# One written order for the lead and the first block of a fused attention and two-MoE kernel, with y of two chunks sent through memory

## Chip, core, metric

The program runs on one core of one Trainium2 chip. The metric is the device time of one execution, in microseconds (us). The profiled execution has a time of its own, and a span from its first to its last instruction.

## What is computed

```python
def _attn_ref(q, k, v, a_re, a_im):               # 4 batches, 8 heads, 768 steps, head size 48
    mag = np.sqrt(a_re * a_re + a_im * a_im)
    scale = np.minimum(mag, 0.999) / (mag + 1e-06)
    a_re_n, a_im_n = (a_re * scale, a_im * scale)
    for t in range(S):
        S_re, S_im = (a_re_n*S_re - a_im_n*S_im + kv[t], a_re_n*S_im + a_im_n*S_re)
        y[:, :, t] = einsum('bhd,bhde->bhe', q[:, :, t], S_re)

def _moe_ref(x, w_in, w_out):                     # 3072 tokens, 384 -> 2048 -> 384
    h = x @ w_in
    sp = np.where(h > 20.0, h, np.log1p(np.exp(np.minimum(h, 20.0))))
    return (h * np.tanh(sp)) @ w_out

def _moe2_ref(x, w_a, w_b, w_out):                # 384 -> 1536 -> 384
    return ((x @ w_a) * (x @ w_b)) @ w_out
# attention, its y as 3072 x 384 tokens into the first MoE, and that into the second
```

## The kernel before, in words

**Attention** is cut into 24 chunks of 128 steps: chunk c = 4j + b is the j-th stretch of batch b. A chunk loads `a` (real and imaginary part), `q`, `k`, `v`. From `a` it makes the size and the angle of the decay: squares (`decay_1`), their sum (`decay_sum`), Ln and Exp, `tangent`, `decay_4` (tile `size`), Arctan (`angle`). Two matmuls with a triangle of ones sum both along the steps (`pl` and `pt`, `running_sum`). `decay_exp` and `scale_qk` scale q and k, `reduce_angle` and `trig` give sine and cosine, and `rotate_one` writes the rotated q and k. Then come transposes (`pqT`, `pkT`), scores (`psc`, masked by a predicated copy into `am` or `before_x`), `values` (y) and `outer` (`pu`, the chunk's share of the state `W`). From chunk 4 on a chunk needs its forerunner's last angle and size, which go through memory (`turn_d`, `end_d`), and its y goes through memory too: both halves `yh` and `yl` are written to `yt_d` and read back as `xh` and `xl`. Chunks 0 to 3 make y with the tokens on the partitions (`pyt`), copy it (`yt`), and turn it by three transposes (`px`).

**The first MoE** works in blocks of 512 tokens (block j = chunks 4j to 4j+3), 16 units in each. A unit is `moe1_h` (9 matmuls into an `hps` buffer; the pool `ps_h` has two), `mish_factor` (one VectorE instruction and four on ScalarE), `mish_product` (VectorE, which gives the `hps` buffer back) and, two units later, `moe1_x2`. In block 0 `moe1_x2` is three full float32 matmuls; in the others nine on split halves. The weights come as 8-byte words; each pair of units needs two loads, each decoded by three VectorE instructions (`wf`, `wout`) and split by one copy on ScalarE (`hi`) and one subtraction on GpSimd (`lo`). **The second MoE** follows.

**The order.** The lead, `lead_in`, is the attention of chunks 0 to 3 in a list of steps whose order `in_order` pins on VectorE (DVE), ScalarE (ACT), TensorE (PE) and GpSimd (POOL), not on the load queue (SP). After it the loop over units calls `do_w` for the next weight step and `run_to` for attention slots, and the Tile scheduler may move what it issues.

```python
        for name in """
            sq0 add0 ln0 sq1 add1 ex0 ln1 sq2 tan0 ex1 sq3 ell0 add2 pl0 ln2 ex2 ep0 ell1 tan1 at1 add3 pl1 d1
            ...
            px3 xh2 xh3 xl2 xl3 tan4
        """.split():
            others[name]() if name in others else steps[name[:-1]](int(name[-1]))
        return pipeline(steps1[4:], 2, w_out_1, w_in_1[1:])
```

Of the kernel before, what the change touches and what calls it, by code (L numbers as in the profile page):

```python
# [21 lines left out]
def kernel(  # L22
# [14 lines left out]
    nc = tc.nc  # L37
# [103 lines left out]

    def load_weights(nm, j, src, pool, place, late=False):
# [13 lines left out]
        def decode(first=True, rest=True):  # L156
            if late and first:
                f[0] = wps[0].tile([P, a, b], F32, tag="f", name=f"w{nm}{j}", bufs=NF // 2 + 1)
                whole[nm, j] = f[0], split
                if src.dtype == F32:  # L160
                    nc.vector.tensor_copy(f[0], raw)
                    return
            if src.dtype != F32:
                if not late and first:
                    f[0] = pool.tile([P, a, b], F32, tag="wf32", name="wf32")
                fu, low, high = f[0].bitcast(U32), raw[..., 0], raw[..., 1]
                if first:
                    nc.vector.tensor_scalar(fu, high, 3, 0x3FFFFFFF, ALU.logical_shift_left, ALU.bitwise_and)
                    nc.vector.scalar_tensor_tensor(fu, high, 0xC0000000, fu, ALU.bitwise_and, ALU.bitwise_or)  # L169
                if rest:  # L170
                    nc.vector.scalar_tensor_tensor(fu, low, 29, fu, ALU.logical_shift_right, ALU.bitwise_or)

        def split():
            hi = place(f"w{nm}h{j}", [P, a, b])
            if late:
                lo = wps[0].tile([P, a, b], F32R, tag="f", name=f"w{nm}l{j}", bufs=NF // 2 + 1)
            else:
                lo = place(f"w{nm}l{j}", [P, a, b])
            weights[nm, j] = [hi, lo]
            act(out=hi, in_=f[0], func=AF.Copy)  # L180
            nc.gpsimd.tensor_tensor(lo, f[0], hi.bitcast(F32), ALU.subtract)
# [79 lines left out]
    def in_rows(c, nm):  # L261

        if c < B:
            return pair(c, nm, nm, "h", "a")
        own = QH if nm == "qh" else KH
        if nm == "qh":
            nc.gpsimd.memset(own[:, :, D:], 0.0)
        st[nm, c] = own.rearrange("p (h a) d -> p h a d", a=2)[..., :D]
        return st[nm, c]

    def decay_1(c):
        act(out=pair(c, "s", "qh", "a", "h"), in_=st["a", c], func=AF.Square)
# [173 lines left out]

    def values(c):
# [4 lines left out]
        if not j:  # L452
# [5 lines left out]
        p = st["py", c] = ps_a.tile([P, HH, C], F32, tag="ps", name="py")  # L458
# [11 lines left out]
    def store_y(c):  # L470
        j, b = chunk(c)
        if not j:
# [8 lines left out]
    def store_y2(c):  # L481
        j, b = chunk(c)
        if not j:
            return
        py, yh, yl = st.pop(("y", c))
        nc.vector.tensor_tensor(yl, py, yh.bitcast(F32), ALU.subtract)
        for y, d in zip((yh, yl), yt_d[j]):
            for par in range(2):
# [3 lines left out]
                )  # L492

# [15 lines left out]

    def state(c):  # L510
        j, b = chunk(c)
        if j == NC - 1:
            return
        Wb = W[b][:, :H * D].rearrange("p (h d) -> p h d", d=D)
        us, g = st.pop(("pu", c)), st.pop(("g", c))
        if j:
            nc.vector.tensor_tensor(Wb, Wb, us, ALU.add)
            us = Wb
        (nc.gpsimd if us is Wb else nc.vector).tensor_tensor(Wb, us, g.to_broadcast([P, H, D]), ALU.mult)
# [3 lines left out]
    def read_x(c):  # L523
# [4 lines left out]
        if not j:  # L528
# [70 lines left out]
    def mish_factor(p):  # L599

        m = mp.tile([P, TN], F32, tag="m", name="m")
        nc.vector.tensor_scalar(m, p, 20.0, None, ALU.min)  # L602
        act(out=m, in_=m, func=AF.Exp)
        act(out=m, in_=m, func=AF.Square, bias=bias_one)
        act(out=m, in_=m, func=AF.Ln, scale=0.2, bias=bias_fifth)
# [554 lines left out]
```

## Time and profile before

| | |
|---|---|
| median of 3 runs | 1092.6 us (1092.25 to 1093.58) |
| the profiled execution | 1091.89 us, its span 1090.2 us |
| busy: PE, DVE, ACT, POOL | 1049.1, 655.7, 610.5, 231.4 us |
| granted clock of TensorE, mean | 0.996 |

PE is busy for 96% of the span. "Idle before" is the time in which an engine waited ahead of an instruction, with what ended the wait.

### The profile page before, as it was taken

What the parts mean: (1) busy time and instruction counts of PE and PEld (TensorE: products, weight loads), DVE (VectorE), ACT (ScalarE), POOL (GpSimd) and SP (SyncE); (2) the same over time, 40 slices, a digit from 0 to 9 for tenths busy, and PEclk for the clock granted to TensorE, in tenths of its full rate; (3) what the DMA queues carried; (4) which work ended last, traced back from release to release, by engine and by line L of the source; (5) the groups of instructions that cost most, each with busy time, mean ns of one, the idle gap of its engine ahead of it and who ended that gap; (6) DMA issues with size and microseconds to landing.
All of it is one profiled execution on the core that took longest, in us unless ns stands there. A gap on an engine that the chain in (4) does not pass through costs nothing.

```text
span 1090.2 us, 15919 instructions
## 1 busy us (share of the span) xinstructions
PE 1049.1 (96%) x6060; PEld 874.8 (80%) x6060; DVE 655.7 (60%) x998; ACT 610.5 (56%) x968; POOL 231.4 (21%) x265
## 2 busy tenths in 40 slices
PE   4979999999999999999999999999999999999997
PEld 1956666788888888888877778888888888888886
DVE  6898976787777777777589998532322322422222
ACT  7868887898788887788767842221221222212211
POOL 2122333444334334333331123100000000000000
PEclk9999999999999999999999999999999999999999
DMA  9656652354444343343155366110100100100000
GB/s 199 140 155 170 166 152 66 67 96 86 112 81 81 67 95 79 83 102 79 31 164 182 126 217 211 44 58 1 30 29 1 58 1 1 44 1 1 29 1 32
DMA packets 203549, 90.92 MB, mean 83 GB/s; under 512 B 144781, under 2 KB 187850, under 8 KB 203466
## 3 DMA queue, kind: packets, MB, share of 16 engines
q1 hardware_dynamic: 202410, 89.62, 32.9%
q8 instruction: 50, 0.82, 0.3%
q10 hardware_dynamic: 1056, 0.21, 0.1%
q14 instruction: 33, 0.27, 0.1%
HBM read 72.44 MB, written 17.36 MB: 82 GB/s over the span
## 4 chain that ended last, share of the span: by engine, by line
PE 72%; DVE 12%; ACT 6%; issue 4%; DMA 3%; POOL 2%; SPq 1%; ACTq 0%; DVEq 0%; POOLq 0%
PE x2ps L639 12%; PE ops L719 12%; PE hps L596 12%; PE psa L694 11%; PE psb L694 11%; PE psc L435 3%; PE py L465 3%; ACT m L59 3%; PE pkT L412 2%; PE pqT L412 2%; DVE wf L169 1%; ACT L54 1%; DVE m L602 1%; PE pt L331 1%; PE pu L504 1%
## 5 line engine op out<-in xcount | busy, mean ns | idle before, releaser
L705 DVE TENSOR_TENSOR a_sb<-a_sb,psb 128x512 f32<-128x512 f32 x72 | 49.4, 686 | 224.6 <-PE psb L694 224.6
L59 ACT ACTIVATE m<-m 128x512 f32<-128x512 f32 x192 | 119.4, 632 | 62.5 <-DVE m L602 57.7
L59 ACT ACTIVATE a_sb<-psa 128x512 f32<-128x512 f32 x72 | 42.9, 596 | 162.8 <-PE psa L694 160.7
L59 ACT ACTIVATE ph<-a_sb 128x512 fp32r<-128x512 f32 x72 | 45.4, 631 | 156.7 <-DVE a_sb L705 156.7
L596 PE MATMUL hps<-xh,winh 128*128 128x512 f32 x288 | 118.9, 414 | 7.8 <-DVE gh L613 6.4
L623 POOL TENSOR_TENSOR gl<-m,gh 128x512 fp32r<-128x512 f32 x64 | 83.2, 1300 | 151.7 <-DVE gh L622 128.4
L596 PE MATMUL hps<-xl,winh 128*128 128x512 f32 x288 | 114.0, 396 | 0.0
L596 PE MATMUL hps<-xh,winl 128*128 128x512 f32 x288 | 113.9, 396 | 0.0
L719 PE MATMUL ops<-woh,ph 128*128 128x384 f32 x288 | 97.1, 337 | 0.0
L719 PE MATMUL ops<-woh,pl 128*128 128x384 f32 x288 | 97.1, 337 | 0.0
L719 PE MATMUL ops<-wol,ph 128*128 128x384 f32 x288 | 96.7, 336 | 0.0
L639 PE MATMUL x2ps<-gl,wouth 128*128 128x512 f32 x240 | 94.3, 393 | 2.2 <-DVE gl L623 1.2
L639 PE MATMUL x2ps<-gh,wouth 128*128 128x512 f32 x240 | 94.1, 405 | 1.8 <-ACT gh L59 1.5
L639 PE MATMUL x2ps<-gh,woutl 128*128 128x512 f32 x240 | 94.0, 392 | 0.0
L616 DVE SCALAR_TENSOR_TENSOR m<-m,hps 128x512 f32<-128x512 f32 x80 | 54.7, 684 | 62.3 <-ACT m L59 61.5
L694 PE MATMUL psa<-xh,wal 128*128 128x512 f32 x216 | 85.2, 394 | 0.0
L694 PE MATMUL psa<-xl,wah 128*128 128x512 f32 x216 | 85.1, 394 | 0.0
L694 PE MATMUL psa<-xh,wah 128*128 128x512 f32 x216 | 84.4, 391 | 0.6 <-DVE a_sb L705 0.6
L694 PE MATMUL psb<-xh,wbh 128*128 128x512 f32 x216 | 84.2, 390 | 0.0
L694 PE MATMUL psb<-xh,wbl 128*128 128x512 f32 x216 | 84.2, 390 | 0.0
L694 PE MATMUL psb<-xl,wbh 128*128 128x512 f32 x216 | 84.2, 390 | 0.0
L707 DVE TENSOR_TENSOR pl<-a_sb,ph 128x512 fp32r<-128x512 f32 x72 | 52.0, 722 | 39.0 <-ACT ph L59 39.0
(167 smaller groups left out, 2335.8 us busy)
## 6 DMA issues: line engine op xcount, KB each, us to landing
wraw<-in_moe_w_out_dram SPq DMA_DIRECT2D x14, 768.0 KB
wraw<-in_moe_w_in_dram SPq DMA_DIRECT2D x8, 768.0 KB
a<-in_a_re_dram SPq DMA_DIRECT2D x24, 192.0 KB
q<-in_q_dram SPq DMA_DIRECT2D x24, 192.0 KB
k<-in_k_dram SPq DMA_DIRECT2D x24, 192.0 KB
v<-in_v_dram SPq DMA_DIRECT2D x24, 192.0 KB
wraw<-in_moe_w_a_dram SPq DMA_DIRECT2D x6, 768.0 KB
wraw<-in_moe_w_b_dram SPq DMA_DIRECT2D x6, 768.0 KB
```

What stands on the lines that cost most here:

```text
L59: x = nc.scalar.activation(**kw)
L412: nc.tensor.transpose(p[:, i, :], src[:, h].rearrange("p a d -> p (a d)") if c < B else own[:, h], ident)
L435: nc.tensor.matmul(p[:, i, :], lhsT=st["kT", c, hf][:, i, :], rhs=st["qT", c, hf][:, i, :], start=True, stop=True)
L465: nc.tensor.matmul(p[par * 64:(par + 1) * 64, i, :], lhsT=w[:, col:col + 64], rhs=x[:, first + par, :], start=(n == 0), stop=(n == len(ter ...
L596: nc.tensor.matmul(p, lhsT=w[:, kk, :], rhs=x[:, kk, :], start=(i == 0), stop=(i == len(ops) - 1))
L616: nc.vector.scalar_tensor_tensor(m, m, 2.5, p, ALU.subtract, ALU.mult)
L623: (nc.vector if on_act else nc.gpsimd).tensor_tensor(gl, m, gh.bitcast(F32), ALU.subtract)
L639: nc.tensor.matmul(x2ps[m], lhsT=w[:, ms], rhs=x, start=(f == 0 and i == 0), stop=(f == NF - 1 and i == len(terms) - 1),)
L694: nc.tensor.matmul(p, lhsT=w[:, kk, :], rhs=x[:, kk, :], start=(i == 0), stop=(i == len(ops) - 1))
L705: nc.vector.tensor_tensor(a_sb, a_sb, pb, ALU.mult)
L707: nc.vector.tensor_tensor(lo, a_sb, hi.bitcast(F32), ALU.subtract)
L719: nc.tensor.matmul(ops_t[t], lhsT=x[:, tsl], rhs=w, start=(f == 0 and i == 0), stop=(f == NF2 - 1 and i == 2),)
```

## The change

Lead, block 0 and the first two units of block 1 are one list of names, which `run` turns into steps. Each engine keeps the list's order, the load queue SP now too. A name like `rq2` is a step of chunk 2; a name with a dot is one of a weight load (`w.3` issues load 3; `da`, `dc`, `db` are its three decodes, `hi` and `lo` its split; `so`, `sl` split a kept w_out) or of a unit (`h.0`, `mn`, `ma`, `mb`, `pr`, `x.0`). So weight decodes, unit 0 and the attention of chunks 4 to 9 stand where the list has them. Three other things are new: y of chunks 0 and 1 is made as column tiles and sent through memory, as it is for later chunks; the squares of chunks 1 to 3 run on DVE instead of ACT; and the kept w_out tiles have a buffer by name (`kept`) instead of nine that go round.

```diff
     def decay_1(c):
+        if c in (1, 2, 3):
+            nc.vector.tensor_tensor(pair(c, "s", "qh", "a", "h"), st["a", c], st["a", c], ALU.mult)
+            return
         act(out=pair(c, "s", "qh", "a", "h"), in_=st["a", c], func=AF.Square)
...
+    BY_MEMORY = (0, 1)
     def values(c):
-        if not j:
+        if not j and c not in BY_MEMORY:
             p = st["py", c] = ps_l.tile([P, H, D], F32, tag="pl", name="pyt")
...
-            terms = [(W[b], qT[hf]), (vt, am[hf])]
+            terms = [(W[b], qT[hf]), (vt, am[hf])] if j else [(vt, scored(c)[hf])]
...
-    weights1 = lead_in()
-    last, after_lead = in_order(first, (E.DVE, E.Activation, E.PE, E.Pool)), traced()
+    run("""
+            a0 sq0 add0 a1 sq1 add1 ln0 ex0 tan0 at0 a2 sq2 add2 ln2 ex2 ln1 ex1 ell0 pl0 ep0 w.1 da.1 dc.1
+            ...
+            xh3 ht3 xl3 close da.4 at5 cy5 ca5 ep5 dc.4 db.4 ou2 tk14 ck14 tq14 cq14 io1 h.0 mn.0 ma.0 w.5
+            da.5 re2 dc.5 db.5 pt5 h.1 mn.1 tk04 ou3 mb.0 pr.0 he5 w.6 a6 re5 st2 st3 open so.0 sl.0 ma.1 mb.1
+            ...
+    """)
+    last, after_lead = in_order(first, (E.DVE, E.Activation, E.PE, E.Pool, E.SP)), traced()
+    slot[0] = 50
...
-    for ui in range(len(units) + lag):
-        if ui == 3:
-            behind(after_lead, last)
+    for ui in range(18, len(units) + lag):
```

**TensorE, end of the lead and the first units.** Before (`pu` is `outer`; `hps` with `winh_476` is units 0 and 1, with `winh_585` units 2 and 3; `x2ps` is `moe1_x2`; the last `pl` and `pt` are chunk 4's):

```order
L532 MATMUL px<-ident,yt 128x128 x6
L504 MATMUL pu<-v,kh 64x48 x11
L596 MATMUL hps<-xh,winh_476 128x512 x2
L504 MATMUL pu<-v,kh 64x48 x6
...
L331 MATMUL pl<-size,csum 128x384
L504 MATMUL pu<-v,kh 64x48 x47
L331 MATMUL pt<-a,tsum 128x384
L596 MATMUL hps<-xh,winh_585 128x512
...
L639 MATMUL x2ps_801<-gh,wout_485 128x512
```

and after the change, from chunk 5's `pl` on (`winh_208` is units 0 and 1, `winh_325` units 2 and 3):

```order
L349 MATMUL pl<-size,csum 128x384
L568 MATMUL px<-ident,yt 128x128 x6
L534 MATMUL pu<-v,kh 64x48 x16
L434 MATMUL pkT<-ident,khp 128x128 x4
L434 MATMUL pqT<-ident,qhp 128x128 x4
L632 MATMUL hps<-xh,winh_208 128x512
...
L349 MATMUL pt<-a,tsum 128x384
...
L434 MATMUL pkT<-ident,khp 128x128 x4
L534 MATMUL pu<-v,kh 64x48 x16
L434 MATMUL pqT<-ident,qhp 128x128 x4
L632 MATMUL hps<-xh,winh_325 128x512
...
L688 MATMUL x2ps_859<-gh,wout_264 128x512
```

Three chunks' `pu`, chunk 4's sums and half its transposes, and chunk 5's `pl` now stand ahead of unit 0; behind unit 1 stand 4 + 16 + 4 small matmuls ahead of unit 2.

**VectorE, between the last `xl` of block 0 and the first instructions of the units** (`L602`, later `L638`, reads `hps`). Before:

```order
L544 TENSOR_TENSOR xl<-px,xh 128x3x128 x2
L291 TENSOR_TENSOR a<-a,khp 128x384
L297 TENSOR_SCALAR qhp<-qhp 128x384
L298 SCALAR_TENSOR_TENSOR size<-khp,qhp 128x384
L168 TENSOR_SCALAR wout_611<-wraw 128x768
L519 TENSOR_TENSOR W_129<-pu,g 128x384
L169 SCALAR_TENSOR_TENSOR wout_611<-wraw,wout_611 128x768
L168 TENSOR_SCALAR wf_627<-wraw 128x768
L171 SCALAR_TENSOR_TENSOR wout_611<-wraw,wout_611 128x768
L169 SCALAR_TENSOR_TENSOR wf_627<-wraw,wf_627 128x768
L602 TENSOR_SCALAR m<-hps 128x512
```

and after the change:

```order
L300 TENSOR_TENSOR a<-a,khp 128x384
L415 TENSOR_TENSOR qhp<-q,a 128x16x48
L415 TENSOR_TENSOR khp<-k,a 128x16x48
L580 TENSOR_TENSOR xl<-px,xh 128x3x128 x2
L172 TENSOR_SCALAR wout_690<-wraw 128x768
L321 SCALAR_TENSOR_TENSOR a<-size,a 1x384
L174 SCALAR_TENSOR_TENSOR wout_690<-wraw,wout_690 128x768
L176 SCALAR_TENSOR_TENSOR wout_690<-wraw,wout_690 128x768
L638 TENSOR_SCALAR m<-hps 128x512
L172 TENSOR_SCALAR wf_749<-wraw 128x768
L174 SCALAR_TENSOR_TENSOR wf_749<-wraw,wf_749 128x768
```

Nine instructions stood between them before, four now; chunk 4's rotation (`L415`) and chunk 5's `tangent` (`L300`) have gone ahead of the last `xl`.

**The load queue, between the last loads of the lead and unit 0.** Before (`g` is the read of `end_d`, `size<-turn_d` the read of the carried angle):

```order
L153 DMA wraw<-in_moe_w_in_dram 128x3x512
L308 DMA size<-turn_d_90 1x384
L220 DMA q<-in_q_dram 128x8x48
L220 DMA k<-in_k_dram 128x8x48
L220 DMA a<-in_a_re_dram 128x8x48
L220 DMA a<-in_a_im_dram 128x8x48
```

and after the change, from the second read of chunk 4's `g` on:

```order
L396 DMA g<-end_d_86 48x8x1 x2
L316 DMA size<-turn_d_91 1x384
L572 DMA xh<-yt_dh_68 128x3x128
L572 DMA xl<-yt_dl_69 128x3x128
L157 DMA wraw<-in_moe_w_in_dram 128x3x512
L396 DMA g<-end_d_88 48x8x1 x2
```

The read of chunk 1's `xh` and `xl`, which did not exist before, stands behind the read of chunk 5's carried angle; chunk 0's stands three rows ahead of these.

## Rows read from the trace of the kernel before

**Rows 1.** The page: busy time by engine.
```profile
PE 1049.1 (96%) x6060; PEld 874.8 (80%) x6060; DVE 655.7 (60%) x998; ACT 610.5 (56%) x968; POOL 231.4 (21%) x265
```

**Rows 2.** Windows up to 180 us: PE, PEld, DVE, ACT, POOL busy; clock; DMA.
```profile
0.00:5.90 5.90, 0.00 (x0) 0.00 (x0) 0.12 (x3) 2.12 (x2) 5.26 (x18) 1.00 0.86 134
5.90:13.60 7.70, 3.06 (x4) 1.00 (x4) 5.01 (x12) 6.87 (x10) 1.25 (x7) 1.00 1.27 236
13.60:52.78 39.18, 33.26 (x239) 28.01 (x238) 33.98 (x56) 33.44 (x58) 2.21 (x10) 1.00 0.84 154
66.40:83.89 17.49, 15.55 (x42) 9.92 (x43) 17.01 (x27) 10.19 (x15) 3.13 (x2) 0.80 0.44 141
```

**Rows 3.** Windows from unit 0's first matmul on, to 180 us and beyond.
```profile
52.78:180.00 127.22, 118.65 (x769) 81.49 (x767) 107.05 (x152) 96.98 (x147) 37.74 (x34) 0.97 0.58 150
180.00:330.00 150.00, 145.70 (x1045) 121.73 (x1044) 112.95 (x183) 129.41 (x207) 63.93 (x80) 1.00 0.42 88
330.00:1090.20 760.20, 748.47 (x4011) 642.60 (x4009) 396.61 (x595) 341.62 (x550) 120.98 (x118) 1.00 0.24 66
```

**Rows 4.** What PE waited for: us in total, times, longest.
```profile
PE hps L596 <- DVE gh L613: 6.4, 3, 3.3
```

**Rows 5.** Timeline of PE: start, us, instruction, idle before.
```profile
25.81 1.06 PE L412 MATMUL pqT<-ident,qhp 128*96 128x128 f32 x4
30.35 0.60 PE L412 MATMUL pqT<-ident,qhp 128*96 128x128 f32 x4
...
66.40 0.50 PE L596 MATMUL hps<-xh,winh 128*128 128x512 f32 x1 [3.33 <-DVE gh L613]
67.07 0.63 PE L596 MATMUL hps<-xh,winl 128*128 128x512 f32 x1
...
72.96 0.39 PE L596 MATMUL hps<-xl,winh 128*128 128x512 f32 x1
...
79.44 0.50 PE L596 MATMUL hps<-xh,winh 128*128 128x512 f32 x1 [1.94 <-DVE gh L613]
```

**Rows 6.** Timeline of DVE around the first units.
```profile
53.52 2.05 DVE L297 TENSOR_SCALAR qhp<-qhp 128x384 f32<-128x384 f32 x1
...
60.09 0.69 DVE L602 TENSOR_SCALAR m<-hps 128x512 f32<-128x512 f32 x1
...
67.13 0.55 DVE L385 TENSOR_TENSOR q<-q,size 128x384 f32<-128x384 f32 x1
67.60 0.95 DVE L171 SCALAR_TENSOR_TENSOR wout<-wraw,wout 128x768 uint32<-128x768 uint32 x1
68.47 0.55 DVE L386 TENSOR_TENSOR k<-k,size 128x384 f32<-128x384 f32 x1
...
78.44 0.35 DVE L297 TENSOR_SCALAR qhp<-qhp 128x384 f32<-128x384 f32 x1
```

**Rows 7.** Timeline of POOL, the split of the second w_in load.
```profile
53.36 1.95 POOL L181 TENSOR_TENSOR winl<-wf,winh 128x768 fp32r<-128x768 f32 x1 [8.80 <-ACT winh L59]
```

**Rows 8.** The chain of waits at full clock: start, us, what.
```profile
87.94 0.44 PE pkT L412 x4
88.38 0.65 PE pt L331 x2
89.02 2.07 PE hps L596 x9
...
92.88 2.58 PE x2ps L639 x6
95.45 1.90 PE py L465 x32
97.35 0.71 PE pu L504 x24
```

**Rows 9.** Load queue: chunk 4's y written and read back.
```profile
98.02 0.30 SPq L489 DMA_DIRECT2D yt_dh<-yh  x1
...
103.89 0.52 SPq L536 DMA_DIRECT2D xh<-yt_dh  x1
```

More of the change, by code (lines that the diff above doesn't have):

```diff
@@ L154, in load_weights, with decode @@
         f = [raw]
-        def decode(first=True, rest=True):
-            if late and first:
-                f[0] = wps[0].tile([P, a, b], F32, tag="f", name=f"w{nm}{j}", bufs=NF // 2 + 1)
+        def decode(part=None):
+            if late and part in (None, 0):
+                f[0] = kept(j, F32, f"w{nm}{j}")
                 whole[nm, j] = f[0], split
-                if src.dtype == F32:
+            if src.dtype == F32:
+                if late and part in (None, 0):
                     nc.vector.tensor_copy(f[0], raw)
[L162 to L181, printed above, removed]
+                return
+            if not late and part in (None, 0):
+                f[0] = pool.tile([P, a, b], F32, tag="wf32", name="wf32")
@@ L830, in behind, with run @@
                 tc.add_manual_dep(x, last[x.engine], no_sync, reason="after the lead")
-    def lead_in():
-        for c in range(B):
-            load_a(c)
-        decode, split = steps1[0]()
-        for c in range(B):
-            load_qk(c)
-        for c in range(B):
-            load_v(c)
-        decode_2, split_2 = steps1[1]()
-        run_to(slot[0] + 1)
-        w_in_1 = steps1[2]()
-        def size(c):
-            decay_4(c)
-            split_ell(c)
+    units = [(b, f) for b in range(NB) for f in range(NF)]
+    ready, lag = {}, 2
+    hs, ms, loads = {}, {}, {}
+    late_pools = {}
+    def run(names):
         def turned(c):
@@ L887, in lead_in @@
-        """.split():
-            others[name]() if name in others else steps[name[:-1]](int(name[-1]))
-        return pipeline(steps1[4:], 2, w_out_1, w_in_1[1:])
+        parts = {
+            "w": lambda n: loads.update({n: steps1[n - 1]()}),
+            "da": lambda n: loads[n][0](0), "dc": lambda n: loads[n][0](1), "db": lambda n: loads[n][0](2),
+            "hi": lambda n: loads[n][1](0), "lo": lambda n: loads[n][1](1),
+            "so": lambda n: whole["out", n][1](0), "sl": lambda n: whole["out", n][1](1),
+            "h": lambda n: hs.update({n: moe1_h(*units[n], ps_h)}),
+            "mn": lambda n: ms.update({n: mish_bound(hs[n])}),
+            "ma": lambda n: mish_grow(ms[n]), "mb": lambda n: mish_shrink(ms[n]),
+            "pr": lambda n: ready.update({n: mish_product(hs.pop(n), ms.pop(n), units[n][0])}),
+            "x": lambda n: moe1_x2(*units[n], *ready.pop(n)),
+        }
@@ new lines, in run, with end_lead, end_first @@
+        for name in names.split():
+            kind, dot, n = name.partition(".")
+            if name in late_pools:
+                late_pools[name]()
+            elif dot:
+                parts[kind](int(n))
+            else:
+                steps[name[:-1]](int(name[-1]))
+    def end_lead():
+        nonlocal mp
+        lead.close()
+        mp = allp.enter_context(tc.tile_pool(name="mp", bufs=3))
+    def end_first():
+        nonlocal ps_x
+        tail.close()
+        ps_x = w1.enter_context(tc.tile_pool(name="ps_x", bufs=1, space=PSUM))
+        wps.append(allp.enter_context(tc.tile_pool(name="wp1", bufs=NF)))
@@ L976 @@
             moe2_out(*units[ui - lag], *pend.pop(ui - lag), ps_o, p2)
+    behind(after_lead, last)
     allp.close()
```

214 lines of the change are left out of this document (131 added, 83 removed).

## The prediction

> **What bounds the kernel now.** First the page: PE is busy 96% of the span, DVE 60%, ACT 56% [rows 1]. PE is the bound, so a change can only win where PE stands idle or runs at its lower clock. The windows say where that is. From 180 us to the end PE is busy 145.7 of 150.0 and 748.5 of 760.2 us [rows 3]. Behind unit 17 both programs have the same number of matmuls (only neighbours change places), so I leave those 910.2 us as they are, with 1.5 us either way for units that start in another state. All else lies in the first 180 us, of which the trace of before makes three parts:
>
> - Up to 52.78 us, where unit 0 starts, PE is idle for 16.5 us and DVE is busy 0.1 + 5.0 + 34.0 = 39.1 us. DVE's idle time there is 5.8 us until the first data, 2.7 us to 13.6 and 5.2 us after that [rows 2].
> - From 52.78 to 180 PE is busy 118.65 of 127.22 us [rows 3], so 8.6 us idle.
> - Inside that, from 66.40 to 83.89, the granted clock is 0.80 on average [rows 2]: after a wait of 3.33 us and again after one of 1.94 us, matmuls that take 0.39 us elsewhere take 0.63 [rows 5]. That is the 1.2 GHz level instead of 2.4, and costs 0.20 x 17.5 = 3.5 us.
>
> The waits of the last two points are mostly one: an `hps` matmul behind `gh`, 6.4 us in 3 times [rows 4]. `ps_h` has two buffers, and a third unit must wait until the first unit's product is made. That product was late since DVE came to unit 0's first instruction only at 60.09 [rows 6], some 5 us after unit 0's matmuls (2.07 us of work from 52.78 on [rows 8], with some of `pu` between them): the decodes of the next two loads and a stalled `L297` stood ahead of it.
>
> So T, the time at which unit 18 starts, is now 52.8 + 115.1 of PE work at full clock (118.65 - 3.5) + 12.1 lost (8.6 + 3.5) = 180.0. A new T is made of the same three terms.
>
> **Term 1: when unit 0 starts.** In the new list it stands behind more work. On DVE the following is new ahead of the last `xl`: the squares of chunks 1 to 3 and chunk 4's rotation, 5 instructions of 128x768; `tangent` of chunks 4 and 5, chunk 4's carried angle, two scalings, chunk 5's sum, two states `W` and two sizes, 10 of 128x384; two `tensor_scalar`, and three of chunk 4's `reduce_angle`; and two `yl` in place of two `xl`. From start to start a 128x384 costs 0.47 us and a 128x768 0.87, a `tensor_scalar` 0.35 when nothing stalls it [rows 6]; for the other three I take 0.5 each, and `yl` against `xl` is worth 0.3. Sum: 4.35 + 4.7 + 0.7 + 1.5 + 0.3 = 11.5 us. So DVE has 39.1 + 11.5 = 50.6 us to do before unit 0. The three squares leave ACT (at 33.4 of 39.2 us nearly as full as DVE in that window [rows 2]).
>
> What idle time comes on top? The 5.8 + 2.7 us at the start stay, since they wait for the first loads: 59.1. The 5.2 us after that are waits of a chunk's next step on PE or ACT; the list puts chunk 4's and 5's steps between those of chunks 2 and 3. If all are filled, unit 0 starts at 59.1, if none at 64.3. I take half: 61.7.
>
> A stall adds to the upper end. `L297` took 2.05 us at 53.52 and 0.35 at 78.44 [rows 6]; the long one ended with the split that POOL ran from 53.36 to 55.31 [rows 7]. Two splits stand in the lead after the change too, so up to 1.7 us more: 66.0. The Trainium skill (GPSIMD Engine Reference, Specifications) says that GpSimd's SBUF interfaces are shared with VectorE, with contention for instructions with two SBUF inputs or in a two-port mode. The trace agrees: 1.7 us lost here. By that rule the new squares, which have two SBUF inputs each and have left ACT, can stall as well, at most for both splits' whole time, 3.9 us, and unit 0 would start at 68.2; by the row it is 66.0.
>
> PE in the lead is no limit at full clock: it was busy 36.3 us before unit 0 [rows 2] and gets 5.1 us more (below), 41.4 of 61.7. y of chunks 0 and 1 by column tiles shortens it (`py` with its two terms takes 1.90 us [rows 8], one term about half, and the transposes fall away), which I count at nothing. What that costs instead is a way through memory: for chunk 4 the first write was issued at 98.02 and the read at 103.89 [rows 9], 5.9 us later. Chunks 0 and 1 are written first in the list and have ten microseconds and more for it, so also nothing, if the queue lets them (rival 3).
>
> **Term 2: PE's work from unit 0 to unit 18.** Moved ahead of unit 0 are 8 transposes (0.44 for 4), two `pl` and one `pt` (0.65 each), and 37 of the 64 `pu` matmuls that stood behind its start (0.71 for 24 records, two records a matmul: 2.2) [rows 8]. That is 0.9 + 1.95 + 2.2 = 5.05. Units cost the same as before: 2.07 for `hps`, 2.58 for `x2ps` [rows 8]. So 115.1 - 5.0 = 110.1.
>
> **Term 3: what PE loses in between.** It lost 12.1 us. The list takes away what made unit 0's product late: only the decode of one load (three instructions, under 2.5 us) stands on DVE between the last `xl` and unit 0's bound, while PE computes unit 0 for 2.07 us; and three small steps (0.44 + 0.95 + 0.44) stand on PE between units 1 and 2, where it stood idle for 3.33. DVE and ACT have room: 107.05 and 96.98 us of work in 127 [rows 3], less what has moved ahead. I take 1.7 us for one stretch at the lower clock, as each of the two before cost, and 1.3 us for waits: 3.0. Bounds: 0 and 12.1.
>
> **Sum.** T = 61.7 + 110.1 + 3.0 = 174.8 instead of 180.0: 5.2 us less. The profiled execution took 1091.89 us, so 1086.7; it lies 0.7 us under the median of the runs shown, which I leave inside the range.
>
> **Rivals.**
>
> 1. *More is filled.* Unit 0 at 59.1 and PE loses nothing: T = 169.2, 1081.1 us. For it: a list that holds loads, decodes and attention together can place each step for all engines. Against it: DVE would have to work without a wait for 46 us, and it was idle 5.2 of 39 so far. Chance 0.20 for a gain of over 8 us.
> 2. *No change.* The 5.2 us of DVE's waits and a POOL stall stay, unit 0 at 66.0, loss 3: T = 179.1, 1091.0 us. An engine that must keep a written order waits for a late step with all behind it. Chance 0.14 for within 0.2% of 1092.6 (2.2 us, about what a measurement of this kernel can tell from no change).
> 3. *Slower: the two `hps` buffers go on holding PE.* All of block 0 is in written order now, on SP too. A weight load waits there for its buffer, and the read of chunk 1's `xh` stands behind the read of chunk 5's angle, which waits for a matmul of the lead. If a late load or decode delays products as before, PE loses 12.1 us again while its start is 9 us later: T = 61.7 + 110.1 + 12.1 = 183.9, 1095.8 us. It decides from a loss of 8.2 us on. For it: three waits of this kind now. Against it: what stood ahead of them has been moved. Chance 0.07.
> 4. *Slower: the clock.* In the lead of before, transposes went from 1.06 us for four at 25.81 to 0.60 at 30.35 [rows 5], the step from 1.2 to 2.4 GHz; before that PE had run with few gaps. The new lead spreads nearly the same PE work over 9 us more. If the clock stayed down until unit 0, the 23 us from 30 to 52.78 would take 46: unit 0 at 13.6 + 33.3 + 5.1 + 23 = 75.0 at worst, T = 188, 1100 us. The Trainium skill (TensorE: Matmul & The Clock Gate, on HAM oscillation) says that an array which pauses between bursts falls back to half rate; rows 5 show that behind both waits. But at half rate PE would have few gaps left in the lead and rise again. Chance 0.04.
>
> **Chances and range.** My forecast, a gain of 2.2 to 8 us (1084 to 1089.7), has 0.55. With rival 1 that is faster 0.75; same 0.14; slower 0.11. The range that leaves out 2 in 10 reaches from rival 1's time, less the 1.5 us for the units behind 18 and a little more, to rival 3's: 1079 to 1095.5.
>
> **What would show it.** In the new profile: unit 0's first `hps` at 59 to 66 us; DVE's busy time ahead of it near 51 us; unit 18's first at 169 to 180; waits of `hps` for `gh` well under 6.4 us and at most one stretch at the lower clock after 60 us; the windows behind unit 18 as before. I am wrong if unit 0 starts past 70, which would be the load queue or the clock; if PE waits for `gh` as often as now; or if units behind 18 wait for attention that the list has left late.

## The result, and the profile after

The changed kernel takes 1108.16 us (median of 4 runs, 1106.77 to 1108.59), the kernel before beside it 1092.42 us: a ratio of 1.0141, 95% interval 1.0123 to 1.0158. It is slower by 15.7 us, where the sum had a gain of 5.2.

First the page, busy time by engine, to be held against [rows 1]:

```profile
PE 1049.0 (95%) x6054; PEld 871.6 (79%) x6054; DVE 662.6 (60%) x1001; ACT 612.2 (55%) x965; POOL 236.5 (21%) x265
```

TensorE's work is the same, VectorE's has grown by 6.9 us, and the span is 16 us longer. The windows of the changed kernel (length; PE, PEld, DVE, ACT, POOL busy; granted clock; DMA share; GB/s) say where. Unit 0's first `hps` starts at 60.2, unit 18's at 196.9:

```profile
0.00:60.20 60.20, 38.87 (x323) 29.10 (x324) 52.55 (x92) 49.91 (x76) 12.80 (x36) 1.00 0.86 167
60.20:120.00 59.80, 50.45 (x257) 32.41 (x256) 57.25 (x71) 42.36 (x62) 22.84 (x15) 0.97 0.51 147
120.00:142.41 22.41, 12.60 (x74) 8.45 (x73) 8.25 (x14) 11.59 (x18) 1.84 (x1) 0.70 0.58 142
142.41:196.90 54.49, 52.98 (x352) 37.20 (x352) 32.77 (x50) 41.03 (x62) 11.50 (x13) 1.00 0.38 84
196.90:1106.30 909.40, 894.12 (x5054) 764.46 (x5052) 511.81 (x778) 467.28 (x750) 187.49 (x201) 1.00 0.28 72
```

Behind unit 18 nothing has changed (909.4 us, 910.2 before). Unit 0 starts 1.5 us ahead of its forecast (61.7). Between them, in 136.7 us instead of 127.2 [rows 3], PE is idle for 136.7 - 116.0 = 20.7 us, in two places of different kinds: from 60 to 120, where DVE is busy for 57.25 of 59.80 us, and from 120 to 142, where nobody is busy and the clock is at 0.70.

What PE, DVE and the load queue (SPq) waited for, from 60 to 200 us (us in total, times, longest):

```profile
PE pu L534 <- DMA v<-in_v_dram: 9.4, 2, 8.0
PE x2ps L688 <- DVE gh L662: 7.1, 4, 3.2
PE hps L632 <- DVE gh L662: 3.4, 3, 2.2
...
DVE wf L172 <- DMA wraw<-in_moe_w_in_dram: 10.8, 1, 10.8
...
SPq L228 <- DVE qhp L415: 27.6, 2, 14.1
```

The wait of [rows 4] has halved (6.4 to 3.4). Two others have come: for `v`, and for `gh` ahead of `x2ps`. The load queue's last row is the key to the first of them; its timeline (start, us, instruction) shows it in place:

```profile
107.15 0.37 SPq L157 DMA_DIRECT2D wraw<-in_moe_w_out_dram  x1
121.12 0.37 SPq L228 DMA_DIRECT2D a<-in_a_re_dram  x1
121.54 0.58 SPq L228 DMA_DIRECT2D a<-in_a_im_dram  x1
122.17 0.51 SPq L387 DMA_DIRECT2D end_d<-size  x1
...
125.74 0.47 SPq L157 DMA_DIRECT2D wraw<-in_moe_w_in_dram  x1
126.31 0.43 SPq L157 DMA_DIRECT2D wraw<-in_moe_w_out_dram  x1
...
127.15 2.02 SPq L247 DMA_DIRECT2D v<-in_v_dram  x1
```

For 13.6 us the queue issues nothing. It stands at the load of chunk 7's `a` (`a7`), whose buffer is free only when DVE has rotated chunk 5's q (`rq5`); loads 15 and 16 and a `v` stand behind it in the list. (The other of the two waits, 14.1 us for chunk 8's `a`, costs next to nothing: it falls behind 142, where PE is idle for 1.5 of 54.5 us.) DVE's timeline has that rotation at 120.09, and then a hole:

```profile
63.19 0.69 DVE L638 TENSOR_SCALAR m<-hps 128x512 f32<-128x512 f32 x1 [0.43 <-DMA g<-end_d]
...
71.76 0.68 DVE L638 TENSOR_SCALAR m<-hps 128x512 f32<-128x512 f32 x1
...
76.87 0.68 DVE L662 SCALAR_TENSOR_TENSOR gh<-m,hps 128x512 f32<-128x512 f32 x1
77.47 1.62 DVE L172 TENSOR_SCALAR wout<-wraw 128x768 uint32<-128x768 uint32 x1
79.13 2.47 DVE L174 SCALAR_TENSOR_TENSOR wout<-wraw,wout 128x768 uint32<-128x768 uint32 x1
81.52 0.68 DVE L638 TENSOR_SCALAR m<-hps 128x512 f32<-128x512 f32 x1
...
120.09 0.95 DVE L415 TENSOR_TENSOR qhp<-q,a 128x768 f32<-128x768 f32 x1
131.80 0.56 DVE L172 TENSOR_SCALAR wf<-wraw 128x768 uint32<-128x768 uint32 x1 [10.76 <-DMA wraw<-in_moe_w_in_dram]
```

The first row is unit 0's bound, its first instruction on DVE. The rows from 71.76 to 81.52 show the other place. A decode at 77.47 takes 1.62 us and one at 79.13 takes 2.47, where their like take 0.56 (at 131.80) and, as in [rows 6], 0.95. POOL at that time:

```profile
71.02 2.50 POOL L188 TENSOR_TENSOR winl<-wf,winh 128x768 fp32r<-128x768 f32 x1 [1.58 <-ACT winh L59]
...
76.11 2.57 POOL L188 TENSOR_TENSOR woutl<-wout,wouth 128x768 fp32r<-128x768 f32 x1 [2.59 <-ACT kT L59]
78.63 2.15 POOL L188 TENSOR_TENSOR winl<-wf,winh 128x768 fp32r<-128x768 f32 x1
```

Each stretched decode ends about its own length after POOL's subtraction has ended (78.68, 80.78), while `m<-hps` at 71.76, also under a subtraction, keeps its 0.68 us. Unit 3's bound, at 81.52, stood behind both; its matmuls were done at 78.0. PE's timeline has the consequence:

```profile
85.81 2.84 PE L688 MATMUL x2ps<-gh,wout 128*128 128x512 f32 x6 [3.19 <-DVE gh L662]
...
89.19 0.39 PE L632 MATMUL hps<-xh,winh 128*128 128x512 f32 x1
...
97.25 0.50 PE L632 MATMUL hps<-xh,winh 128*128 128x512 f32 x1 [2.23 <-DVE gh L662]
...
98.05 0.62 PE L632 MATMUL hps<-xh,winh 128*128 128x512 f32 x1
...
134.13 1.95 PE L534 MATMUL pu<-v,khp 128*64 128x48 f32 x32 [8.04 <-DMA v<-in_v_dram]
```

Behind the wait of 2.23 us the matmuls of 0.39 us take 0.62 for a while (1.2 instead of 2.4 GHz), as in [rows 5]; behind that of 3.19 us they keep 0.39. The long stretch at the lower level falls into the hole from 120 to 142 (0.70 in the windows).

So two theories. **A**: the load queue in written order makes the hole from 120 to 142 us. **B**: DVE is full from 60 to 120 us, so bounds and products come late. A rival within B asks what fills it: decodes that the list has too early, or the stretches under POOL.

### The profile page after: what moved, and what is told of

It is laid out like the page before. It is cut to its first block, busy times and chain, and to the rows that moved or that the text cites. A ratio compares the mean times of both kernels' runs of the same rounds, so it can differ in the third digit from the quotient of the medians.

```text
span 1106.3 us, 15891 instructions
## 1 busy us (share of the span) xinstructions
PE 1049.0 (95%) x6054; PEld 871.6 (79%) x6054; DVE 662.6 (60%) x1001; ACT 612.2 (55%) x965; POOL 236.5 (21%) x265
## 4 chain that ended last, share of the span: by engine, by line
PE 64%; DVE 13%; ACT 7%; DMA 6%; issue 6%; POOL 2%; SPq 1%; DVEq 0%; ACTq 0%; POOLq 0%
PE ops L772 12%; PE psa L747 12%; PE psb L747 12%; PE x2ps L688 11%; PE hps L632 9%; ACT m L59 3%; PE py L490 3%; PE psc L457 2%; PE pkT L434 1%; DVE wf L176 1%; DVE m L638 1%; PE pqT L434 1%; ACT L54 1%; DVE wf L174 1%; PE pu L534 1%
## 5 line engine op out<-in xcount | busy, mean ns | idle before, releaser
L758 DVE TENSOR_TENSOR a_sb<-a_sb,psb 128x512 f32<-128x512 f32 x72 | 49.4, 686 | 224.8 <-PE psb L747 224.8
```

Of the source, the lines that this page charges most:

```text
L758: nc.vector.tensor_tensor(a_sb, a_sb, pb, ALU.mult)
```

## The experiments

All medians in one table, with the ratio to the kernel before run beside them. That one's median was 1092.42 us beside the changed kernel, 1090.94 beside 1 to 4, 1091.26 beside 5 to 8, and 1090.57 to 1090.86 beside the others, so between these groups a difference is good to a microsecond or so only. "Unit 0" and "unit 18" are the starts of their first `hps` in the profiled execution, and PE busy is what the window between them says. A profiled execution is one of several: that of 9 took 1.9 us more than the median, that of 10 took 3.4 us less.

| kernel | median us | ratio (95%) | unit 0 | unit 18 | between | PE busy |
|---|---|---|---|---|---|---|
| changed | 1108.16 | 1.0141 (1.0123 to 1.0158) | 60.2 | 196.9 | 136.7 | 116.0 |
| 1 `a7` later | 1097.62 | 1.006 (1.0043 to 1.0077) | 60.4 | 187.2 | 126.8 | 114.0 |
| 2 queue free | 1096.94 | 1.006 (1.0043 to 1.0077) | 60.2 | 185.5 | 125.3 | 113.6 |
| 3 decodes later | 1116.83 | 1.0243 (1.0225 to 1.0261) | 60.2 | 204.8 | 144.6 | 115.5 |
| 4 ten decode steps out | 1087.79 | 0.9972 (0.996 to 0.9983) | 60.2 | 176.0 | 115.8 | 110.7 |
| 5 = 2 + 3 | 1110.13 | 1.0169 (1.015 to 1.0188) | 60.1 | 201.1 | 141.0 | 120.0 |
| 6 eleven subtractions out | 1086.69 | 0.996 (0.9946 to 0.9974) | 60.1 | 176.8 | 116.7 | 110.9 |
| 7 squares on ACT | 1100.85 | 1.009 (1.0073 to 1.0107) | 64.1 | 190.5 | 126.4 | 115.5 |
| 8 y without memory | 1102.97 | 1.0124 (1.0101 to 1.0147) | 64.7 | 191.0 | 126.3 | 115.3 |
| 9 quarters | 1091.86 | 1.0008 (0.9999 to 1.0017) | 60.0 | 182.5 | 122.5 | 112.8 |
| 10 six swaps | 1097.38 | 1.0056 (1.0042 to 1.007) | 60.1 | 184.5 | 124.4 | 112.8 |
| 11 subtractions on DVE | 1109.60 | 1.0176 (1.0162 to 1.0191) | 60.4 | 198.4 | 138.0 | 118.8 |
| 12 before, eleven out | 1086.06 | 0.9955 (0.9941 to 0.997) | 52.4 | 173.0 | 120.6 | 116.1 |
| 13 = 10 + all quarters | 1090.77 | 0.9997 (0.9988 to 1.0007) | 61.2 | 181.1 | 119.9 | 112.5 |
| 14 before, quarters | 1088.78 | 0.998 (0.997 to 0.9989) | 52.4 | 177.9 | 125.5 | 118.0 |
| 15 eighths | 1092.78 | 1.0017 (1.0008 to 1.0027) | 60.1 | 181.5 | 121.4 | 112.6 |
| 16 all quarters | 1091.61 | 1.0005 (0.9995 to 1.0014) | 61.7 | 181.7 | 120.0 | 112.4 |
| 17 three steps ahead | 1093.30 | 1.0024 (1.0014 to 1.0034) | 60.3 | 183.1 | 122.8 | 114.1 |

### 1 and 2. The load queue

```diff
-dc.13 pr.6 db.13 w.14 a7 yt4 pl6 ep6 he6 re6 h.7 mn.7
+dc.13 pr.6 db.13 w.14 yt4 pl6 ep6 he6 re6 h.7 mn.7
...
-so.5 so.6 cq05 cq15 w.15 w.16 da.15
+so.5 so.6 cq05 cq15 w.15 w.16 a7 da.15
```

> The changed kernel with one entry of the list moved: the load of chunk 7's `a` stands behind chunk 5's `rotate` (just behind the load w.16) instead of before it, so that the load queue no longer waits for that buffer with w.15, w.16, `v` and the `g` reads behind it. Theory A (the written order of the load queue makes the hole from 120 to 142 us): unit 18 starts some 13 us earlier than 196.9 (9.8 us of PE's idle time and 3.3 of its lower clock go), so 1093 to 1097 us, DVE's wait of 10.8 us for the load in L172 and PE's wait of 8.0 us for `v` are gone, and PE's loss before 120 us, about 11, stays. Theory B (DVE is full in block 0 since decodes stand units ahead of their use, and that sets the pace throughout): the DVE work comes later by what the hole was, gain under 3 us, 1105 us or more.

```diff
-    last, after_lead = in_order(first, (E.DVE, E.Activation, E.PE, E.Pool, E.SP)), traced()
+    last, after_lead = in_order(first, (E.DVE, E.Activation, E.PE, E.Pool)), traced()
```

> The changed kernel with the load queue (SP) taken out of the engines that keep the list's order; the four other engines keep it. Theory A: the load of chunk 7's `a` no longer holds up the loads behind it, the hole from 120 to 142 us goes, so 1093 to 1097 us as with the load moved. If the written order of the queue served for something else (loads that now go ahead take a transfer's place), it is less. Theory B: under 3 us of gain, 1105 us or more.

One name moved in the list takes 10.5 us off (9.1 if each is counted from the kernel before beside it; unit 18 starts 9.7 earlier), and the free queue 11.2. Theory A holds. The hole is gone from the queue of the first (timeline; load 15 now goes at 111.56 instead of 125.74):

```profile
111.56 0.41 SPq L157 DMA_DIRECT2D wraw<-in_moe_w_in_dram  x1
115.86 0.39 SPq L157 DMA_DIRECT2D wraw<-in_moe_w_out_dram  x1
120.02 0.37 SPq L228 DMA_DIRECT2D a<-in_a_re_dram  x1
```

What is left is the loss before 120 us. PE's waits in the first kernel, from 60 to 200 us:

```profile
PE x2ps L688 <- DVE gh L662: 8.0, 6, 3.2
PE hps L632 <- DVE gh L662: 1.4, 2, 1.2
```

### 3 and 5. Loads and decodes later

```diff
-w.8 da.8 dc.8 h.3 mn.3 db.8 h.4 mn.4 x.2
+w.8 h.3 mn.3 h.4 mn.4 da.8 dc.8 db.8 w.10 x.2
...
-w.12 da.12 dc.12 mb.5 pr.5 hi.11 lo.11 so.3 h.6 mn.6
+mb.5 pr.5 so.3 h.6 mn.6 da.10 dc.10 db.10 w.12
```

(Shown are two of nine places. The decodes of the weights 8 to 16 go one to five units later in the list, most of them two or three; their loads move less, and those of weights 10 and 11 stand a little earlier than they did.)

> The load of `a` of chunk 7 behind chunk 5's `rotate`, that of chunk 8 behind chunk 6's, and the loads and decodes of the weights 8 to 16 written two to three units later, just ahead of the unit that first needs them; all else as in the changed kernel. Theories A and B together: the hole from 120 to 142 us goes (13 us), and with DVE's decodes out of the way the waits of `hps` and `x2ps` between 80 and 120 us shrink from about 11 to 5 us or less: 1085 to 1091 us. A alone: as with the load of chunk 7 moved alone, 1093 to 1097. If the late decodes come too late, `hps` waits for its weight and the time is over 1097.

Far off: 19 us slower than with chunk 7's load moved alone, where 6 to 12 less was expected. With the queue in written order, `v` now stands behind weight loads that wait for their decodes; of PE's waits (from 60 to 200 us) the longest kind is

```profile
PE pu L534 <- DMA v<-in_v_dram: 18.5, 2, 11.5
```

So the same edit with a free queue:

> The kernel with the later loads and decodes of weights 8 to 16, now with the load queue (SP) free of the list's order (the two edits of the two earlier runs together). If the later decodes themselves were right and only the queue, in written order, held `v` back behind weight loads (PE waited 7.0 and 11.5 us for `v` in that run): PE's waits for `v` are gone and the gaps of `hps` and `x2ps` between 80 and 120 us are down to half, 1087 to 1092 us, against 1096.9 for the free queue alone. If not the place of the decodes but DVE's total of work in block 0 sets the pace: 1095 to 1098 us. If late decodes make units wait for their weights: over 1098 us.

PE no longer waits for `v`, but the time is still 13 us over that of the free queue alone. DVE is less busy (40.4 us from 60 to 120) and PE loses more. So the decodes of the changed kernel are not simply too early. A weight must go from DVE through ACT's copy and POOL's subtraction before PE can use it, and POOL now waits for the copies; but no wait of PE names a weight, its longest are for `gh` (POOL, then PE, from 60 to 200 us). What delays `gh` there is not shown:

```profile
POOL winl L188 <- ACT winh L59: 37.7, 5, 18.6
...
PE x2ps L688 <- DVE gh L662: 10.2, 4, 3.9
```

### 4 and 6. What fills DVE

```diff
-... db.6 ... da.6 dc.6 so.1 db.6 so.2 ...
+... db.6 ... da.6 so.1 db.6 so.2 ...
```

(The same for `dc.5` to `dc.14`; `a8` also stands behind `rq6`.)

> The load of `a` of chunks 7 and 8 behind the `rotate` that frees its buffer, and the second of the three decode steps (the sign bit of the weight) left out for weights 5 to 14: 10 DVE instructions, about 9 us of DVE's work between 60 and 120 us; these weights lose their sign. Theory B (DVE sets the pace there): 5 to 9 us less than with chunk 7's load moved alone, 1085 to 1090 us, and PE's idle time between 60 and 120 us at 5 us or less. Theory A alone (the rest of the loss comes from the order, not from DVE's load): within 2 us of the kernel with chunk 7's load moved, 1093 to 1097 us.

The time falls by 9.8 us, and unit 18 starts 11.2 us earlier than in the first run. B holds. But the ten steps are only some 9.5 us of it: DVE is busy for 15.1 us less between unit 0 and unit 18 (99.86 against 84.79, below), so about 5.6 us of stretches went with them, and this run alone does not tell work from stretches. Then the stretches alone, with all decodes in place:

```diff
+            if part == 1 and nm + str(j) in ("in2", ..., "in6", "out0", ..., "out5"):
+                weights[nm, j].append(weights[nm, j][0])
-            if part in (None, 1):
+            elif part in (None, 1):
```

> The kernel with chunk 7's load moved, and POOL's subtraction that makes a weight's low part left out for the weights of eleven loads that units 4 to 13 use (their high part is used twice; 11 POOL instructions of about 2 us). Seven DVE instructions between 60 and 120 us were 9.8 us longer in all than their like, each while such a subtraction ran. If those stalls are a large part of what fills DVE: they vanish, DVE does the same work about 9 us sooner, unit 18 starts 8 to 11 us earlier than 187.2, 1086 to 1090 us. If DVE's own work sets the pace and the stalls only take its spare time: under 3 us of gain, 1095 us or more.

10.9 us, as much as the whole of B. No DVE instruction has been taken out here, only POOL's subtractions beside them. Windows from unit 0 to unit 18, of the first run, then of 4, then of 6:

```profile
60.40:187.20 126.80, 114.02 (x681) 75.51 (x679) 99.86 (x133) 95.02 (x141) 35.67 (x29) 0.99 0.51 130
```
```profile
60.20:176.00 115.80, 110.67 (x681) 75.41 (x679) 84.79 (x123) 94.57 (x141) 34.19 (x29) 1.00 0.55 142
```
```profile
60.10:176.80 116.70, 110.91 (x682) 75.51 (x680) 87.72 (x133) 94.95 (x141) 12.00 (x17) 1.00 0.56 142
```

DVE's 133 instructions take 99.86 us with the subtractions beside them and 87.72 without, and the way from unit 0 to unit 18 is 10.1 us shorter. A rival would be that PE had waited for the low parts themselves, which 6 does not make; but in the first run no wait of PE between unit 0 and unit 18 names a weight's low part. PE runs at full clock in both of the lower rows, which also gives its true work: 110.7 to 110.9 us.

### 7 and 8. The two other parts of the change undone

```diff
     def decay_1(c):
-        if c in (1, 2, 3):
+        if False:
```

> The kernel with chunk 7's load moved, and the squares of chunks 1 to 3 back on ACT: one part of the change undone. By the first term of the prediction they cost DVE 3 x 0.87 = 2.6 us ahead of unit 0: unit 0 at 57.8 instead of 60.4 if DVE sets the start of unit 0, and 1095 us; if ACT, busy 50 of 60 us there, takes them as late as DVE did, unit 0 stays at 60.4 or goes up to 63 and the time is 1097.5 to 1100 us.

```diff
-    BY_MEMORY = (0, 1)
+    BY_MEMORY = ()
...
-cq12 xl0 ell4 re0 a5 sq5 sy0 cy4 ou0
+cq12 px0 xh0 xl0 ell4 re0 a5 sq5 cy4 ou0
```

(The same for chunk 1; the writes and reads of both, `sy` and `io`, are out.)

> The kernel with chunk 7's load moved, and y of chunks 0 and 1 made as for chunks 2 and 3, by transposes on PE and copies on ACT, without the way through memory: the other part of the change undone, the list otherwise as it was. If the way through memory is hidden and spares PE and ACT work in the lead: unit 0 starts 1 to 3 us later than 60.4, 1098.5 to 1100.5 us. If the writes and reads of y hold loads up in the queue: unit 0 at 58 to 60, 1094 to 1097 us.

Both parts do good in this list, which was written for them: undone, unit 0 starts 3.7 and 4.3 us later, unit 18 3.3 and 3.8, and the times are 3.2 and 5.4 us longer. The size of neither was foreseen. With the squares on ACT it is DVE that waits for them, at 12.29 and again at 20.26 in its timeline:

```profile
12.29 0.56 DVE L285 TENSOR_TENSOR s<-s 128x384 f32<-128x384 f32 x1 [2.01 <-ACT s L59]
...
20.26 0.56 DVE L285 TENSOR_TENSOR s<-s 128x384 f32<-128x384 f32 x1 [2.65 <-ACT s L59]
```

### 9, 11 and 15. POOL's subtraction in pieces, or on DVE

```diff
-                nc.gpsimd.tensor_tensor(lo, f[0], weights[nm, j][0].bitcast(F32), ALU.subtract)
+                low = [t.rearrange("p a b -> p (a b)") for t in (lo, f[0], weights[nm, j][0].bitcast(F32))]
+                for q in range(0, 2 * DM, DM // 2):
+                    nc.gpsimd.tensor_tensor(*(t[:, q:q + DM // 2] for t in low), ALU.subtract)
```

(As it is for the eleven loads; the others keep one whole subtraction.)

> The kernel with the free load queue, and each of POOL's eleven subtractions for the low parts of the weights of units 4 to 13 (128x768, some 2 us) written as four of 128x192. In all traces so far a stretched DVE instruction ends when POOL's instruction ends. If POOL holds DVE off for one instruction at a time, DVE can go on after a quarter: each stretch falls from about 1.5 us to 0.5 or less, and DVE's instructions on PSUM hide some; 3 to 8 us less than 1096.9. If every quarter stops DVE anew, the stretches add up to the same: 1095 to 1099 us.

5.1 us less, nothing left out: the changed kernel is level with the one before. The two decodes that took 1.62 and 2.47 us take 0.92 and 1.24 (timeline of DVE, then of POOL):

```profile
77.27 0.92 DVE L172 TENSOR_SCALAR wout<-wraw 128x768 uint32<-128x768 uint32 x1
78.22 1.24 DVE L174 SCALAR_TENSOR_TENSOR wout<-wraw,wout 128x768 uint32<-128x768 uint32 x1
...
75.89 4.02 POOL L192 TENSOR_TENSOR woutl<-wout,wouth 128x192 fp32r<-128x192 f32 x4 [2.71 <-ACT kT L59]
```

POOL pays: four quarters take 4.02 us instead of 2.57. Eighths (`DM // 4`) buy no more:

> The kernel with the free load queue, and the eleven subtractions in eight pieces of 128x96 instead of four of 128x192. If the stretch of a DVE instruction is the rest of one POOL instruction, it halves again (0.3 to 0.4 us each with four pieces): 0.5 to 2 us less than with four, 1090 to 1091.5 us. If POOL's cost for each instruction and for its turns (four pieces took 3.0 to 4.0 us instead of 2) grows as fast: low parts come late and it is 1093 us or more.

1092.8 us, within 1 us of the quarters. DVE's work falls from 93.4 to 88.9 us between unit 0 and unit 18, POOL's grows from 49.4 to 59.0, and the time does not follow DVE any more. In place of the stretches DVE's decodes now wait for POOL, three times and 4.0 us in all, where the quarters have one such wait of 0.3 (waits of DVE from 60 to 185 us; the `memset` of `v` stands right behind a subtraction on POOL):

```profile
DVE wf L172 <- POOL winl L192: 2.3, 2, 2.0
...
DVE wf L172 <- POOL v L250: 1.7, 1, 1.7
```

The subtractions on DVE (`nc.vector` for the eleven):

> The kernel with the free load queue, and the eleven low parts of the weights of units 4 to 13 made by DVE instead of POOL; nothing left out. DVE then has 11 instructions of about 0.95 us (10.5 us) more to do and no stretched ones (seven to nine, 9.8 us between 60 and 120 us). If the stretches cost what they show, the two sums are alike: 1095 to 1099 us. If the stretches cost less than work does (DVE has spare time at them), it is slower: 1100 us or more; if they cost more, 1092 or less.

12.7 us slower than with them on POOL: the second outcome, but not for the reason given there. DVE is busy for only 42.8 of 59.6 us up to 120. It stands, in written order, at subtractions whose target buffer PE has not freed yet, a wait that POOL could stand before (waits of DVE from 60 to 150 us):

```profile
DVE woutl L190 <- PE x2ps L690: 11.4, 3, 4.4
```

### 10, 13, 16 and 17. Places in the list

```diff
-w.8 da.8 dc.8 h.3 mn.3 db.8 h.4 mn.4
+w.8 da.8 h.3 mn.3 dc.8 h.4 mn.4 db.8
...
-rk5 cy6 ca6 dc.13 pr.6 db.13
+rk5 pr.6 cy6 ca6 dc.13
```

(Two of six.)

> The kernel with the free load queue, and six local swaps in the list: the bound or the product of units 3 to 10 goes ahead of one or two decode steps (or of ca6, add7, rk6) that stood just before it on DVE, and the last two steps of unit 8's factor ahead of two weight copies on ACT. No work is left out. If PE's waits from 82 to 142 us come from single bounds and products that stand behind stalled decodes: the six gaps (3.2 + 1.0 + 0.5 + 1.8 + 1.4 + 1.2 = 9.1 us) shrink by 6 to 9 us and with them the 1.7 us at the lower clock behind the first: 1087 to 1091 us. If DVE's total sets the pace there and a place in the list only moves the wait: 1095 to 1098 us.

The median does not move (1093.96 to 1099.10; the profiled execution is near the lower end). All subtractions in quarters, without and with the swaps:

> The kernel with the free load queue, and POOL's subtractions for all of `w_in` and `w_out` in four pieces (those of the lead and of weights 13 and later too, which were whole in the run with eleven). Three stretches are left in whole ones: 1.7 us at 16.6, 0.8 at 34.1, and 1.6 at 132.6, ahead of PE's wait of 2.3 us for `gh` at 136.7. If those are on the path: unit 0 starts up to 2 us earlier and that wait shrinks, 1087.5 to 1090.5 us. If they are not: 1091 to 1092.5 us as with eleven.

> The kernel with the free load queue, with the six local swaps in the list, and with POOL's subtractions for the low parts of all of `w_in` and `w_out` in four pieces of 128x192. If the swaps failed alone since stretched instructions took the place of what was moved, they are worth something now: 2 to 5 us less than with the pieces alone, 1085 to 1089 us. If a swap moves a wait from one unit to the next in any case: within 1.5 us of the pieces alone.

Both are level with the kernel before, and 0.8 us apart. In the lead the quarters cost: unit 0 starts at 61.7 and 61.2. At last two products and a rotation further ahead (shown is the first; the lead's splits are whole again):

```diff
-ma.4 ht5 sin5 w.9 w.10 ... add6 ln6 sc5 da.10 dc.10 db.10 h.5 mn.5 s04 cp04 mb.4 pr.4
+ma.4 mb.4 ht5 sin5 w.9 w.10 ... pr.4 add6 ln6 sc5 da.10 dc.10 db.10 h.5 mn.5 s04 cp04
```

> The kernel with free load queue, swaps and pieces, with three more steps moved ahead: unit 4's product (and the two last steps of its factor on ACT) from behind load 10's decode and unit 5's bound to in front of them, unit 1's product ahead of a decode step and unit 2's bound, and chunk 5's `rotate` of q ahead of four instructions of other steps. The splits of the lead are whole again (unit 0 at 60.1 instead of 61.2). PE's gaps that this answers to were 2.7, 1.3 and 1.7 us. If the rest of the loss is single steps that stand too late: these go, unit 18 starts at 174.5 to 176.5 instead of 181.1, 1084 to 1087 us. If DVE's work as a whole sets the pace and a wait only moves on: 1088.5 to 1091 us.

Slower by 2.5 us than 13. The three waits of 13 are gone from where they stood, and three others, larger in sum, stand elsewhere (PE, from 60 to 185 us):

```profile
PE pt L353 <- DVE a L325: 3.5, 1, 3.5
PE pkT L438 <- ACT qT L59: 2.5, 1, 2.5
PE hps L636 <- DVE gh L666: 1.6, 1, 1.6
```

### 12 and 14. The same on the kernel before

> The kernel before, without POOL's subtractions for the weights of eleven loads (the same as in the run of the changed kernel without them: the high part is used twice). In it 14 DVE instructions before 185 us were stretched by 15.2 us in all. If such stretches delay its units as they do those of the changed kernel (11 us there): 1080 to 1084 us, and the change lost nothing by them that it had not lost before. If before they fell on DVE's spare time: 1088 us or more, and the change has brought them onto the path.

(The edits are those of 6 and of 9, in `split` of the kernel before.) 4.8 us: the kernel before loses by the stretches too, by the medians less than half as much (10.9 in the changed kernel), by the windows of one execution each two thirds as much (6.6 against 10.1 us). Window from unit 0 to unit 18, which was 127.22 us [rows 3]:

```profile
52.40:173.00 120.60, 116.06 (x768) 80.46 (x767) 98.81 (x152) 96.51 (x147) 15.71 (x23) 0.99 0.60 159
```

> The kernel before, with POOL's subtractions for the same eleven loads in four pieces of 128x192 each; all else as before. Leaving them out gave it 4.8 us. If POOL holds DVE off for one instruction at a time here too, as in the changed kernel, where pieces gave 5.1 of 11 us: 2 to 4 us of gain, 1087 to 1089 us. If the longer total time of POOL's pieces (some 3.5 us instead of 2) makes low parts late where the kernel before needs them soon: 1091 to 1094 us.

1088.78 us, ratio 0.998 (0.997 to 0.9989), nothing left out: the only complete version here that is faster than both kernels, and it is the old one with POOL's subtractions in quarters.

## Why the prediction was wrong

The sum was made of four pieces, and three of them hold.

- *Behind unit 18*: 910.2 us forecast, 909.4 measured.
- **Term 1**, unit 0's start: 61.7 forecast, 60.2 measured. Two sizes in it were off and cancelled, which is luck: DVE's work ahead of unit 0 is 52.55 us (50.6 forecast), its idle time 7.65 (8.5 + 2.6 = 11.1 forecast), less even than the first rival's 8.5. Nor does the sum say why: the way through memory, counted at nothing, is worth 4.3 us, and the squares, counted as 2.6 us of cost, are worth 3.7, since DVE would have to wait for ACT.
- **Term 2**, PE's work up to unit 18: 110.1 forecast, 110.7 to 110.9 measured at full clock.
- **Term 3**, what PE loses in between: 3.0 forecast with bounds of 0 and 12.1, and 136.7 - 110.8 = 25.9 measured. This is the step that failed.

What it says of unit 0 holds: the bound comes 3.0 us after unit 0's start (63.19) and not 7.3 us, and the waits of `hps` for `gh` are down from 6.4 to 3.4 us. But `x2ps` now waits for `gh` too, so that PE waits for `gh` 7 times and 10.5 us in all against 3 and 6.4, which the prediction itself had named as a sign that it is wrong.

"DVE and ACT have room: 107.05 and 96.98 us of work in 127" is the sentence that fails. It takes a mean over the whole stretch: in the first 59.2 us from unit 0 on the kernel before had 55.36 us of DVE work, and the changed kernel has 57.25 in 59.80. The window of before (as in [rows 2]):

```profile
52.80:112.00 59.20, 53.23 (x345) 36.78 (x345) 55.36 (x85) 45.36 (x69) 13.27 (x12) 0.94 0.63 174
```

And it leaves out what the list does to that work. By the two traces (each instruction's time less that of its shortest like), stretches are some 15 and 14 us up to unit 18 in the two kernels, but in these first 60 us 4 in the kernel before and 11 in the changed one, where the list has put nine of POOL's subtractions in place of five. DVE's own work there has become less, 46 us instead of 51; the stretches have taken the room. The load queue, the other part of the loss, was at nothing in Term 3 and stood only in the third rival. And the upper bound, the loss of before, bounds nothing once the order is another.

What took its place, by the runs: 9.9 us are the queue (136.7 to 126.8 with `a7` moved); 10.1 us are DVE's instructions stretched under POOL (126.8 to 116.7 without the subtractions); 5.9 us are left. Each is the difference of two profiled executions. Against the kernel before, whose loss was 12.1 us and 6.6 of it such stretches (127.2 to 120.6), the queue is new and the stretches weigh 3.5 us more. With 7.4 for the later start and 4.3 less of PE work that gives 7.4 - 4.3 + 9.9 + 3.5 + 0.4 (the rest: 5.9 against 5.5) = 16.9 us, the 196.9 against 180.0 of unit 18.

Of the rivals, the third had the sign and the queue ("A weight load waits there for its buffer"), and rightly said that over 8.2 us lost means slower. It failed in price, by taking 12.1 us again, and in its mechanism: not the two `hps` buffers hold PE but `v` and a decode, behind a load whose buffer a later DVE step frees. It had a chance of 0.07. The fourth did not come: ahead of unit 0 the granted clock is 1.00, and four transposes take 0.60 us from 32.67 on. What it says of [rows 5] is in those rows for the first of the two waits only, as the row at 79.44 is the last one shown; the trace has matmuls of 0.61 to 0.63 us from 80.48 on, behind the second. Stalls under POOL were counted in Term 1 for the lead's two splits alone (at most 3.9 us); of the splits behind unit 0, where [rows 7] shows one of the kind, none was counted.

Open is what holds the last 9 to 12 us in the kernels with quarters. Swaps in the list only moved the waits (10, 17), and with eighths DVE has as little to do as without the subtractions (88.9 and 87.7 us) while the way to unit 18 is 4.7 us longer. DVE's 4.0 us of waits for POOL point to POOL's longer chain, but no run took that alone, and in the quarters it is 0.3 us only.

## What to carry to other kernels

When a load queue joins a written order, go through its DMAs one by one and ask which step frees each buffer: a load written ahead of that step holds up all loads behind it, here for 13.6 us by one name. Read an engine's room in the stretch that needs it and not as a mean, since DVE had 20 us of it in 127 by the mean, but 3.8 in the first 59 of the kernel before and 2.5 in the first 60 of the changed one; and ask what will run beside it there, since 11 of these 57 us were stretches. And where GpSimd works beside a full VectorE, cut its instructions into pieces: it gave 0.5% to the changed kernel with its free queue, and 0.2% to a kernel that was not otherwise changed.

## What the runs showed of the hardware

A GpSimd subtraction on SBUF holds most of VectorE's instructions until it ends if they work on SBUF alone, and none that reads PSUM. In the changed kernel `wout<-wraw` (128x768, 0.55 us) took 1.47, 1.62, 2.22 and 2.19 us when it began under one; all four `m<-hps` and all three `gh<-m,hps` that did so kept their 0.67 to 0.69. A sum on a single row, `a<-size,a` (1x384, 0.54 us), took 2.17, so it is not the size of VectorE's instruction that counts but what is left of GpSimd's. A held instruction ends about its own length after GpSimd's. A few on SBUF alone kept their time: `mins<-look`, a reduction of one input (1.34 to 1.35 us in all 6 cases), and some that began right at the start of a subtraction, which then was the longer one (`wf<-wraw,wf` 0.94 us at 108.83, under a subtraction of 2.92 us from 108.56 on; others take 1.84). The Trainium skill (GPSIMD Engine Reference, Specifications) names the contention, for instructions with two SBUF inputs or in a two-port mode; that it lasts to the end of GpSimd's instruction, and so can be cut by cutting that, is what the quarters show (1.62 to 0.92, 2.47 to 1.24).
